# Attention scores and outputs of a unit in two blocks on TensorE instead of in pairs of heads

## The chip, the cores and the metric

One Trainium2 chip, one core. The metric is the time on the device in microseconds (us), the median of several runs. All runs told here were fast (granted TensorE clock 0.998 to 1.0). Before: 256.43 us (256.35 to 256.56, 3 runs).

## The reference

A sparse attention feeds a gated feed-forward block. Batch 4, 8 heads, 768 positions, head size 64.

```python
def _attn_ref(q, k, v):
    block, window = (32, 16)
    k_sum = k.reshape(B, H, nb, block, D).max(axis=3)        # 24 block keys
    v_sum = v.reshape(B, H, nb, block, D).mean(axis=3)
    scores_l = scale * q @ k.T          # kept where |i - j| < window
    scores_s = scale * q @ k_sum.T + log(block)
    a = softmax(concat([scores_l masked, scores_s]))
    return a @ concat([v, v_sum])

def _moe_ref(x, w_gate, w_val, w_out, w_res):               # x: 3072 x 512, d_ff 1536
    ffn_out = gelu(x @ w_gate) * (x @ w_val) @ w_out
    return x + sigmoid(x @ w_res) * ffn_out
```

## The kernel before

The 3072 rows are worked in eight units of 384 (half a batch each), numbered 0 to 7. A unit has 12 gate and value tiles (names g, vv, product gvT), then three row tiles of residual gate (r, th) and of the second feed-forward matmul (f, 12 steps each). While unit u does its r and f, the attention of unit u + 1 is slipped in: scores s, exp and mask to P, attention output ao, normalized xn, and xn turned to xT for the next unit's matmuls. I call that stretch the boundary of unit u + 1. PSUM, the memory from which the other engines read TensorE's results, has four rotating banks `ps_mm`, a two-bank tile `ps_s`, and one bank each in `ps_t` and `ps_o`.

One head pair (hp), of four:

```python
        def s_step(u, hp, st, banks=None, tiles=None):
            if tiles:
                s, banks = tiles, True
            elif banks:
                s = [p.tile([128, 512], F32, tag=tag, name="s") for p, tag in banks]
            else:
                s2 = ps_s.tile([128, 2, 512], F32, tag="s", name="s")
                s = [s2[:, hh] for hh in range(2)]
            s_mm(u, hp, [x[:, 0:TU] for x in s])
            P = ppool.tile([128, 2, HT, QT], BF16, tag="P", name="P")
            if banks:
                for hh in range(2):
                    nc.scalar.activation(P[:, hh].rearrange("p t q -> p (t q)"), s[hh][:, 0:TU], AF.Exp,
                                         scale=scale, bias=bias_t[:])
            else:
                nc.scalar.activation(P.rearrange("p a t q -> p a (t q)"), s2[:, :, 0:TU], AF.Exp,
                                     scale=scale, bias=bias_t[:])
            if u:
                Pf = P.rearrange("p a t q -> p (a t) q")
                nc.vector.tensor_mul(Pf, Pf, maskt.unsqueeze(1).to_broadcast([128, 2 * HT, QT]))
            st["P", hp] = P

        def av_step(u, hp, st, pool=ps_o, tag="ao"):
            b, half = u // 2, u % 2
            P = st["P", hp]
            ao = pool.tile([128, NSUB, 2, D + 1], F32, tag=tag, name="ao")
            for sub in range(NSUB):
                for hh in range(2):
                    for e in range(2):
                        t = 2 * sub + e
                        nc.tensor.matmul(ao[64 * e:64 * e + 64, sub, hh, :], P[:, hh, t, :],
                                         vext[b % 2][:, half * HT + t, 2 * hp + hh, 0:D + 1],
                                         start=True, stop=True, skip_group_check=True)
            av_end(hp, st, ao)
# ...
        def av_end(hp, st, ao):
            rz = work.tile([128, NSUB, 2, 1], F32, tag="rz", name="rz")
            nc.vector.reciprocal(rz[:], ao[:, :, :, D:D + 1])
            xn = st["xn"][:, hp].rearrange("p s (h d) -> p s h d", d=D)
            nc.vector.tensor_mul(xn, ao[:, :, :, 0:D], rz.to_broadcast([128, NSUB, 2, D]))

        def xt_step(u, ko, st, pool, tag, copy=nc.vector.tensor_copy):
            xp = pool.tile([128, TU], BF16, tag=tag, name="xp")
            for sub in range(NSUB):
                nc.tensor.transpose(xp[:, sub * 128:(sub + 1) * 128],
                                    st["xn"][:, ko, sub, :], ident[:])
            copy(st["xT"][:, ko, :], xp[:])

        def xt_dma(ko, st):
            nc.sync.dma_start_transpose(out=st["xT"][:, ko].rearrange("d (s k) -> d s k", k=128),
                                        in_=st["xn"][:, ko].rearrange("p s d -> p (s d)"))
```

The order at a boundary (`st` is the unit that ends, `nst` the one that comes). Unit 1 has the first order, units 2 to 7 the second:

```python
        def first_out(u, st, gvT, nst):
            n = u + 1
            other = dict(pool=ps_t, tag="t")
            turn = dict(pool=ps_t, tag="t", copy=nc.scalar.copy)
            s_step(n, 0, nst)
            s_step(n, 1, nst, TO2)
            for sub in range(NSUB):
                res_step(st, sub)
            ffn_step(st, gvT, 0, 0, 4)
            av_step(n, 0, nst)
            av_step(n, 1, nst, **other)
            s_step(n, 2, nst)
            ffn_step(st, gvT, 1, 0, 4)
            ffn_step(st, gvT, 2, 0, 4)
            ffn_step(st, gvT, 0, 4, 8)
            xt_step(n, 0, nst, **turn)
            av_step(n, 2, nst)
            s_step(n, 3, nst)
            ffn_step(st, gvT, 1, 4, 8)
            ffn_step(st, gvT, 2, 4, 8)
            ffn_step(st, gvT, 0, 8, FO)
            xt_step(n, 1, nst, **turn)
            av_step(n, 3, nst)
            ffn_step(st, gvT, 1, 8, FO)
            xt_step(n, 2, nst, **turn)
            xt_step(n, 3, nst, ps_o, "ao")
            end_step(u, st, 0)
            ffn_step(st, gvT, 2, 8, FO)
            end_step(u, st, 1)
            end_step(u, st, 2)

        def mid_out(u, st, gvT, nst):
            n = u + 1
            other = dict(pool=ps_t, tag="t")
            s_step(n, 0, nst)
            s_step(n, 1, nst, TO2)
            res_step(st, 0)
            res_step(st, 1)
            ffn_step(st, gvT, 0, 0, 4)
            av_step(n, 0, nst)
            xt_dma(0, nst)
            av_step(n, 1, nst, **other)
            xt_dma(1, nst)
            s_step(n, 2, nst)
            s_step(n, 3, nst, MM2)
            if n % 2 == 0:
                pool_after(nst["P", 3][0:1, 0, 0, 0:1])
                for i in range(2, 4):
                    vsum_bc(n // 2, 3 * i, 3 * i + 3, nc.gpsimd)
            ffn_step(st, gvT, 0, 4, FO)
            ffn_step(st, gvT, 1, 0, 3)
            av_step(n, 2, nst)
            xt_dma(2, nst)
            av_step(n, 3, nst, **other)
            xt_dma(3, nst)
            end_step(u, st, 0)
            ffn_step(st, gvT, 1, 3, FO)
            res_step(st, 2)
            end_step(u, st, 1)
            ffn_step(st, gvT, 2, 0, FO)
            end_step(u, st, 2)
```

The softmax here doesn't subtract the row's maximum and nothing guards it: scores larger than these inputs give would overflow.

Of the kernel before, what the change touches and what calls it, by code (L numbers as in the profile page):

```python
# [8 lines left out]
F32 = mybir.dt.float32  # L9
BF16 = mybir.dt.bfloat16  # L10
AF = mybir.ActivationFunctionType
# [4 lines left out]
def kernel(  # L16
# [11 lines left out]
    nc = tc.nc  # L28
# [25 lines left out]
    wpool = ctx.enter_context(tc.tile_pool(name="wpool", bufs=1))  # L54
    qk = ctx.enter_context(tc.tile_pool(name="qk", bufs=1))
    work = ctx.enter_context(tc.tile_pool(name="work", bufs=3))
    ppool = ctx.enter_context(tc.tile_pool(name="ppool", bufs=4))
    upool = ctx.enter_context(tc.tile_pool(name="upool", bufs=2))
    ps_mm = ctx.enter_context(tc.tile_pool(name="ps_mm", bufs=4, space=bass.MemoryType.PSUM))
    ps_s = ctx.enter_context(tc.tile_pool(name="ps_s", bufs=1, space=bass.MemoryType.PSUM))  # L60
# [17 lines left out]
    q_nat = const.tile([128, NQ, DM], BF16, name="q_nat")  # L78
    vext = [const.tile([128, NT, H, VP], BF16, name=f"vext{i}") for i in range(2)]
    vsum = [const.tile([128, DM], BF16, name=f"vsum{i}") for i in range(2)]  # L80
    vpart = const.tile([128, DM], BF16, name="vpart")
    w_gate = wpool.tile([128, KO, DFF], BF16, name="w_gate")
    w_val = wpool.tile([128, KO, DFF], BF16, name="w_val")
# [55 lines left out]
    with tc.manual_schedule():  # L139
# [182 lines left out]
# [6 lines that stand above are left out]
                s2 = ps_s.tile([128, 2, 512], F32, tag="s", name="s")  # L328
                s = [s2[:, hh] for hh in range(2)]
            s_mm(u, hp, [x[:, 0:TU] for x in s])  # L330
            P = ppool.tile([128, 2, HT, QT], BF16, tag="P", name="P")
            if banks:
                for hh in range(2):
                    nc.scalar.activation(P[:, hh].rearrange("p t q -> p (t q)"), s[hh][:, 0:TU], AF.Exp,  # L334
                                         scale=scale, bias=bias_t[:])
            else:
                nc.scalar.activation(P.rearrange("p a t q -> p a (t q)"), s2[:, :, 0:TU], AF.Exp,  # L337
                                     scale=scale, bias=bias_t[:])
            if u:
                Pf = P.rearrange("p a t q -> p (a t) q")  # L340
                nc.vector.tensor_mul(Pf, Pf, maskt.unsqueeze(1).to_broadcast([128, 2 * HT, QT]))  # L341
            st["P", hp] = P

        MM2 = ((ps_mm, "mm"),) * 2
        TO2 = ((ps_t, "t"), (ps_o, "ao"))
# [13 lines that stand above are left out]
# [18 lines left out]
# [10 lines that stand above are left out]
# [6 lines left out]
        def gv_mm(ps, w, st, fo, kos):  # L393
            for ko in kos:
                nc.tensor.matmul(ps[:, 0:TU], w[:, ko, fo * 128:(fo + 1) * 128], st["xT"][:, ko, :],  # L395
                                 start=(ko == 0), stop=(ko == KO - 1), skip_group_check=True)

        def gv_end(gvT, fo, g, vv):
            ge = work.tile([128, TU], F32, tag="ge", name="ge")
            nc.scalar.activation(ge[:], g[:, 0:TU], AF.Gelu)  # L400
            nc.vector.tensor_mul(gvT[:, fo, :], ge[:], vv[:, 0:TU])  # L401

        def mm_tile(name):
            return ps_mm.tile([128, 512], F32, tag="mm", name=name)
# [13 lines left out]
            gv_end(gvT, 0, g, vv)  # L418

        def fo_last_two(st, gvT):  # L420
            g = [mm_tile("g"), mm_tile("g")]
            for i in range(2):
                gv_mm(g[i], w_gate, st, FO - 2 + i, range(KO))
            for i in range(2):
                vv = mm_tile("vv")
                gv_mm(vv, w_val, st, FO - 2 + i, range(KO))
                gv_end(gvT, FO - 2 + i, g[i], vv)

        def res_step(st, sub):
            ss = slice(sub * 128, (sub + 1) * 128)  # L430
            r = mm_tile("r")
            for ko in range(KO):
                nc.tensor.matmul(r[:], st["xT"][:, ko, ss], w_res[:, ko, :],  # L433
                                 start=(ko == 0), stop=(ko == KO - 1))
            st["th", sub] = work.tile([128, DM], F32, tag="th", name="th")
            nc.scalar.activation(st["th", sub][:], r[:], AF.Tanh, scale=0.5)  # L436

        def ffn_step(st, gvT, sub, lo, hi):
            ss = slice(sub * 128, (sub + 1) * 128)
            if lo == 0:  # L440
                st["f", sub] = mm_tile("f")
            for fo in range(lo, hi):
                nc.tensor.matmul(st["f", sub][:], gvT[:, fo, ss], w_out[:, fo, :],  # L443
                                 start=(fo == 0), stop=(fo == FO - 1), skip_group_check=True)
# [13 lines left out]
        def end_step(u, st, sub):  # L458
            end_part(u, st, sub, st["f", sub], slice(0, DM))
# [122 lines left out]
        def pool_after(x):  # L582
            nc.gpsimd.tensor_copy(gate2[:], x)

        def first_out(u, st, gvT, nst):
            n = u + 1
            other = dict(pool=ps_t, tag="t")
            turn = dict(pool=ps_t, tag="t", copy=nc.scalar.copy)
            s_step(n, 0, nst)
            s_step(n, 1, nst, TO2)  # L590
            for sub in range(NSUB):
                res_step(st, sub)
            ffn_step(st, gvT, 0, 0, 4)
            av_step(n, 0, nst)
            av_step(n, 1, nst, **other)
            s_step(n, 2, nst)
            ffn_step(st, gvT, 1, 0, 4)
            ffn_step(st, gvT, 2, 0, 4)
            ffn_step(st, gvT, 0, 4, 8)
            xt_step(n, 0, nst, **turn)  # L600
            av_step(n, 2, nst)
            s_step(n, 3, nst)
            ffn_step(st, gvT, 1, 4, 8)
            ffn_step(st, gvT, 2, 4, 8)
            ffn_step(st, gvT, 0, 8, FO)
            xt_step(n, 1, nst, **turn)
            av_step(n, 3, nst)
            ffn_step(st, gvT, 1, 8, FO)
            xt_step(n, 2, nst, **turn)
            xt_step(n, 3, nst, ps_o, "ao")  # L610
            end_step(u, st, 0)
            ffn_step(st, gvT, 2, 8, FO)
            end_step(u, st, 1)
            end_step(u, st, 2)

        def mid_out(u, st, gvT, nst):
            n = u + 1
            other = dict(pool=ps_t, tag="t")
            s_step(n, 0, nst)
            s_step(n, 1, nst, TO2)  # L620
            res_step(st, 0)
            res_step(st, 1)
            ffn_step(st, gvT, 0, 0, 4)
            av_step(n, 0, nst)
            xt_dma(0, nst)
            av_step(n, 1, nst, **other)
            xt_dma(1, nst)
            s_step(n, 2, nst)
            s_step(n, 3, nst, MM2)
            if n % 2 == 0:  # L630
                pool_after(nst["P", 3][0:1, 0, 0, 0:1])
                for i in range(2, 4):
                    vsum_bc(n // 2, 3 * i, 3 * i + 3, nc.gpsimd)
            ffn_step(st, gvT, 0, 4, FO)
            ffn_step(st, gvT, 1, 0, 3)
            av_step(n, 2, nst)
            xt_dma(2, nst)
            av_step(n, 3, nst, **other)
            xt_dma(3, nst)
            end_step(u, st, 0)  # L640
            ffn_step(st, gvT, 1, 3, FO)
            res_step(st, 2)
            end_step(u, st, 1)
            ffn_step(st, gvT, 2, 0, FO)
            end_step(u, st, 2)
# [101 lines left out]
```

## Time and profile before

| | before |
|---|---|
| time, median | 256.43 us |
| span of the profiled run | 254.6 us |
| TensorE busy | 97% |
| boundary of unit 1, first s to first g of unit 1 | 13.50 us |
| first s of unit 2 to first s of unit 3 | 28.19 us |

The busy time of each engine in two stretches, the two of the last rows of the table. Columns: the stretch, its length, then busy us and number of instructions of TensorE (PE), its weight loads (PEld), VectorE, ScalarE and GpSimd; then granted clock, DMA share and GB/s:

```profile
38.15:51.65 13.50, 13.24 (x155) 7.17 (x158) 6.92 (x18) 8.13 (x13) 4.68 (x6) 1.00 1.63 190
69.79:97.98 28.19, 27.93 (x238) 15.58 (x241) 15.98 (x31) 13.72 (x24) 15.86 (x21) 1.00 1.16 109
```

TensorE has no idle time to speak of in either, and the others are half idle. Yet "busy" counts a matmul from its start to its modelled end, with the pipeline's overlap.

### The profile page before, as it was taken

What the parts mean: (1) busy time and instruction counts of PE and PEld (TensorE: products, weight loads), DVE (VectorE), ACT (ScalarE), POOL (GpSimd) and SP (SyncE); (2) the same over time, 40 slices, a digit from 0 to 9 for tenths busy, and PEclk for the clock granted to TensorE, in tenths of its full rate; (3) what the DMA queues carried; (4) which work ended last, traced back from release to release, by engine and by line L of the source; (5) the groups of instructions that cost most, each with busy time, mean ns of one, the idle gap of its engine ahead of it and who ended that gap; (6) DMA issues with size and microseconds to landing.
All of it is one profiled execution on the core that took longest, in us unless ns stands there. A gap on an engine that the chain in (4) does not pass through costs nothing.

```text
span 254.6 us, 5847 instructions
## 1 busy us (share of the span) xinstructions
PE 246.6 (97%) x2303; PEld 139.7 (55%) x2328; DVE 159.4 (63%) x364; ACT 129.6 (51%) x216; POOL 97.3 (38%) x128
## 2 busy tenths in 40 slices
PE   6999999999999999999999999999999999999994
PEld 2676555565545665446544665446545555456544
DVE  6985796397667544858567544958567544854424
ACT  8885468366572337353572337254572337353320
POOL 8895542361506970274406970274404000000000
PEclk9999999999999999999999999999999999999999
DMA  5999999999404999399404999289604400230003
GB/s 80 177 182 197 197 205 207 175 176 222 61 19 121 159 150 150 56 161 171 103 18 120 162 155 153 49 162 170 104 18 115 98 3 0 50 139 0 3 1 124
DMA packets 98107, 29.34 MB, mean 115 GB/s; under 512 B 83224, under 2 KB 94944, under 8 KB 97984
## 3 DMA queue, kind: packets, MB, share of 16 engines
q0 software_dynamic: 68352, 14.76, 66.3%
q1 hardware_dynamic: 29728, 14.21, 25.7%
q8 instruction: 18, 0.29, 0.5%
q14 instruction: 9, 0.07, 0.1%
HBM read 29.36 MB, written 6.29 MB: 140 GB/s over the span
## 4 chain that ended last, share of the span: by engine, by line
PE 93%; DVE 5%; issue 2%; DVEq 0%
PE g L395 25%; PE vv L395 24%; PE f L443 23%; PE r L433 8%; PE s L317 3%; PE ao L355 3%; PE vs L282 1%; PE ao L367 1%; PE tp L220 1%; PE vs L290 1%; DVE ks L237 1%; PE xp L380 1%; DVE o L452 1%; DVE th L449 1%; PE gv L395 1%
## 5 line engine op out<-in xcount | busy, mean ns | idle before, releaser
L401 DVE TENSOR_TENSOR gvT<-ge,vv 128x384 bf16<-128x384 f32 x95 | 52.2, 552 | 48.1 <-PE vv L395 43.9
L400 ACT ACTIVATE ge<-g 128x384 f32<-128x384 f32 x95 | 46.7, 491 | 67.3 <-DVE gvT L401 34.8
L395 PE MATMUL g<-xT,w_gate 128*128 128x384 bf16 x380 | 78.0, 326 | 0.0
L395 PE MATMUL vv<-xT,w_val 128*128 128x384 bf16 x380 | 77.8, 326 | 0.0
L443 PE MATMUL f<-w_out,gvT 128*128 128x512 bf16 x262 | 62.7, 379 | 1.5 <-issue 1.1
L395 PEld LDWEIGHTS <-w_gate 128*128 128x128 bf16 x384 | 37.1, 98 | 26.2 <-issue 1.4
L395 PEld LDWEIGHTS <-w_val 128*128 128x128 bf16 x384 | 37.6, 98 | 24.7
L443 PEld LDWEIGHTS <-gvT 128*128 128x128 bf16 x276 | 25.7, 98 | 29.5
L107 POOL DMA_DIRECT2D vext<-in_v_dram x32 | 24.1, 777 | 15.0 <-DMA w_out<-in_moe_w_out_dram 5.6
L436 ACT ACTIVATE th<-r 128x512 f32<-128x512 f32 x24 | 13.5, 607 | 27.6 <-PE r L433 27.6
L449 DVE SCALAR_TENSOR_TENSOR th<-th,f 128x512 f32<-128x512 f32 (+2 forms) x26 | 16.6, 640 | 14.4 <-PE f L443 14.4
L341 DVE TENSOR_TENSOR P<-P,maskt 128x768 bf16<-128x768 bf16 x28 | 16.2, 580 | 11.0 <-ACT P L337 6.1
L433 PE MATMUL r<-w_res,xT 128*128 128x512 bf16 x88 | 22.7, 380 | 0.4
L302 POOL COPY vext<-vsum 32x1536 bf16<-32x1536 bf16 x12 | 17.2, 1464 | 13.0 <-DMA vsum<-vpart 12.9
L452 DVE SCALAR_TENSOR_TENSOR o<-th,xn 128x512 f32<-128x512 f32 (+2 forms) x26 | 18.2, 701 | 0.9
L375 DVE TENSOR_TENSOR xn<-ao,rz 128x384 bf16<-128x384 f32 x32 | 17.8, 557 | 1.1
L337 ACT ACTIVATE P<-s,bias_t 128x768 bf16<-128x768 f32 x17 | 15.3, 901 | 4.5 <-PE s L317 4.3
L127 POOL DMA_DIRECT2D q_nat<-in_q_dram x18 | 15.8, 899 | 0.9 <-issue 0.7
L334 ACT ACTIVATE P<-s,bias_t 128x384 bf16<-128x384 f32 x30 | 15.7, 579 | 0.0
L237 DVE TENSOR_REDUCE ks<-kW 128x24 bf16<-128x768 bf16 x16 | 15.1, 943 | 0.0
L433 PEld LDWEIGHTS <-xT 128*128 128x128 bf16 x96 | 8.8, 98 | 9.9
L373 DVE RECIPROCAL rz<-ao 128x6 f32<-128x6 f32 x32 | 6.1, 191 | 10.9 <-PE ao L355 10.0
(90 smaller groups left out, 187.1 us busy)
## 6 DMA issues: line engine op xcount, KB each, us to landing
out_dram<-o SPq DMA_DIRECT2D x23, 256.0 KB, 2.2
vext<-in_v_dram POOLq DMA_DIRECT2D x32, 96.0 KB, 6.4
q_nat<-in_q_dram POOLq DMA_DIRECT2D x18, 128.0 KB, 6.4
w_gate<-in_moe_w_gate_dram POOLq DMA_DIRECT2D x6, 256.0 KB, 8.9
w_val<-in_moe_w_val_dram POOLq DMA_DIRECT2D x6, 256.0 KB, 9.3
w_out<-in_moe_w_out_dram POOLq DMA_DIRECT2D x3, 512.0 KB, 14.4
k_nat<-in_k_dram POOLq DMA_DIRECT2D x16, 96.0 KB, 5.8
vext<-vext SPq DMA_DIRECT2D x6, 144.0 KB, 5.4
```

Of the source, the lines that this page charges most:

```text
L107: nc.gpsimd.dma_start(out=vext[b % 2][0:QT, :, h, 0:D], in_=v[b, h].rearrange("(t p) d -> p t d", p=QT))
L237: nc.vector.tensor_reduce(out=ks.rearrange("d (t n) -> d t n", n=2), in_=kw[:, :, 0:QT].rearrange("d t (n w) -> d t n w", w=BLK), axis=myb ...
L302: eng.tensor_copy(vext[b % 2][96:128, lo:hi, :, 0:D], src)
L341: nc.vector.tensor_mul(Pf, Pf, maskt.unsqueeze(1).to_broadcast([128, 2 * HT, QT]))
L375: nc.vector.tensor_mul(xn, ao[:, :, :, 0:D], rz.to_broadcast([128, NSUB, 2, D]))
L395: nc.tensor.matmul(ps[:, 0:TU], w[:, ko, fo * 128:(fo + 1) * 128], st["xT"][:, ko, :], start=(ko == 0), stop=(ko == KO - 1), skip_group_ch ...
L400: nc.scalar.activation(ge[:], g[:, 0:TU], AF.Gelu)
L401: nc.vector.tensor_mul(gvT[:, fo, :], ge[:], vv[:, 0:TU])
L433: nc.tensor.matmul(r[:], st["xT"][:, ko, ss], w_res[:, ko, :], start=(ko == 0), stop=(ko == KO - 1))
L443: nc.tensor.matmul(st["f", sub][:], gvT[:, fo, ss], w_out[:, fo, :], start=(fo == 0), stop=(fo == FO - 1), skip_group_check=True)
L449: nc.vector.scalar_tensor_tensor(th[:, cs], th[:, cs], 1.0, f[:, 0:n], ALU.add, ALU.mult)
L452: nc.vector.scalar_tensor_tensor(o.rearrange("p (k d) -> p k d", d=128), th[:, cs].rearrange("p (k d) -> p k d", d=128), 0.5, x, ALU.mult, ...
```

## The change

All scores of a unit are computed in one place: 24 (head pair, query tile) columns in three groups of eight, each filling two banks with 512 columns. All attention outputs are computed in a second place. The aim is to change less often between TensorE's kinds of work. P becomes one tile `p_all` of the whole unit. In unit 1, where x is turned by TensorE, the four transposes stand together. The gelus of the last two tiles are recorded ahead of the value matmuls. Cut to its core:

```diff
+        def s_all(u):
+            # three groups: banks of ps_mm, of ps_s, of ps_t and ps_o
+            for i in range(3):
+                ...
+                for j in range(8):
+                    hp, t = divmod(8 * i + j, HT)
+                    for hh in range(2):
+                        nc.tensor.matmul(s[hh][:, j * QT:(j + 1) * QT], kw[ps, tt, hp, :], ...)
+                ... # exp of 512 columns a bank (1024 in group 1), mask of 512 a head
+        def av_all(u, st):
+            for hp in range(NP):
+                ... # ao: ps_t, ps_o, then the two halves of ps_s; av_end after hp 0, 1 and 3
+                if u > 1: xt_dma(i, st)
         def first_out(u, st, gvT, nst):
+            s_all(n)
+            res_step(st, 0)
+            res_step(st, 1)
+            for lo in (0, 4):
+                for sub in range(2):
+                    ffn_step(st, gvT, sub, lo, lo + 4)
+            av_all(n, nst)
+            for sub in range(2):
+                ffn_step(st, gvT, sub, 8, FO)
+                end_step(u, st, sub)
+            res_step(st, 2)
+            ffn_step(st, gvT, 2, 0, 4)
+            xt_step(n, 0, nst, ps_t, "t", nc.scalar.copy)
+            xt_step(n, 1, nst, ps_o, "ao")
+            xt_step(n, 2, nst, ps_t, "t", nc.scalar.copy)
+            xt_step(n, 3, nst, ps_o, "ao")
+            ffn_step(st, gvT, 2, 4, FO)
             end_step(u, st, 2)
         def mid_out(u, st, gvT, nst):
+            s_all(n)
+            ... # block sums of v to GpSimd, as before
             res_step(st, 0)
             res_step(st, 1)
+            ffn_step(st, gvT, 0, 0, FO)
+            av_all(n, nst)
             end_step(u, st, 0)
+            ffn_step(st, gvT, 1, 0, FO)
             res_step(st, 2)
             end_step(u, st, 1)
             ffn_step(st, gvT, 2, 0, FO)
```

More of the change, by code (lines that the diff above doesn't have):

```diff
@@ L56 @@
     work = ctx.enter_context(tc.tile_pool(name="work", bufs=3))
-    ppool = ctx.enter_context(tc.tile_pool(name="ppool", bufs=4))
     upool = ctx.enter_context(tc.tile_pool(name="upool", bufs=2))
@@ L80 @@
     vsum = [const.tile([128, DM], BF16, name=f"vsum{i}") for i in range(2)]
+    p_all = const.tile([128, 2, NP * HT, QT], BF16, name="p_all")
     vpart = const.tile([128, DM], BF16, name="vpart")
@@ L330, in s_step @@
             s_mm(u, hp, [x[:, 0:TU] for x in s])
-            P = ppool.tile([128, 2, HT, QT], BF16, tag="P", name="P")
+            P = p_all[:, :, hp * HT:(hp + 1) * HT]
             if banks:
@@ L339, in s_step @@
             if u:
-                Pf = P.rearrange("p a t q -> p (a t) q")
-                nc.vector.tensor_mul(Pf, Pf, maskt.unsqueeze(1).to_broadcast([128, 2 * HT, QT]))
+                nc.vector.tensor_mul(P, P, maskt.unsqueeze(1).unsqueeze(1).to_broadcast([128, 2, HT, QT]))
             st["P", hp] = P
+        def s_all(u):
+            b, half = u // 2, u % 2
+            kw, qt = kW[b % 2], qT[b % 2]
+            s2 = None
+            for i in range(3):
+                if i == 0:
+                    s = [ps_mm.tile([128, 512], F32, tag="mm", name="s") for _ in range(2)]
+                elif i == 1:
+                    s2 = ps_s.tile([128, 2, 512], F32, tag="s", name="s")
+                    s = [s2[:, hh] for hh in range(2)]
+                else:
+                    s = [p.tile([128, 512], F32, tag=tag, name="s") for p, tag in TO2]
+                for j in range(8):
+                    hp, t = divmod(8 * i + j, HT)
+                    tt = half * HT + t
+                    for hh in range(2):
+                        ps = slice(hh * 64, hh * 64 + 64)
+                        nc.tensor.matmul(s[hh][:, j * QT:(j + 1) * QT], kw[ps, tt, hp, :],
+                                         qt[ps, tt // 2, hp, (tt % 2) * QT:(tt % 2 + 1) * QT],
+                                         start=True, stop=True, skip_group_check=True)
+                js = slice(8 * i, 8 * i + 8)
+                m = maskt.unsqueeze(1).to_broadcast([128, 8, QT])
+                for hh in range(1 if i == 1 else 2):
+                    if i == 1:
+                        nc.scalar.activation(p_all[:, :, js].rearrange("p a j q -> p a (j q)"), s2[:], AF.Exp,
+                                             scale=scale, bias=bias_t[:])
+                    else:
+                        nc.scalar.activation(p_all[:, hh, js].rearrange("p j q -> p (j q)"), s[hh][:], AF.Exp,
+                                             scale=scale, bias=bias_t[:])
+                for hh in range(2):
+                    nc.vector.tensor_mul(p_all[:, hh, js], p_all[:, hh, js], m)
@@ new lines, in av_all @@
+        def av_all(u, st):
+            b, half = u // 2, u % 2
+            aos = []
+            for hp in range(NP):
+                if hp < 2:
+                    pool, tag = TO2[hp]
+                    ao = pool.tile([128, NSUB, 2, D + 1], F32, tag=tag, name="ao")
+                else:
+                    if hp == 2:
+                        s2 = ps_s.tile([128, 2, 512], F32, tag="s", name="ao")
+                    ao = s2[:, hp - 2, 0:NSUB * 2 * (D + 1)].rearrange("p (s h d) -> p s h d", s=NSUB, h=2)
+                for sub in range(NSUB):
+                    for hh in range(2):
+                        for e in range(2):
+                            t = 2 * sub + e
+                            nc.tensor.matmul(ao[64 * e:64 * e + 64, sub, hh, :], p_all[:, hh, hp * HT + t, :],
+                                             vext[b % 2][:, half * HT + t, 2 * hp + hh, 0:D + 1],
+                                             start=True, stop=True, skip_group_check=True)
+                aos.append(ao)
+                if hp != 2:
+                    for i in range(2 if hp == 3 else hp, hp + 1):
+                        av_end(i, st, aos[i])
+                        if u > 1:
+                            xt_dma(i, st)
@@ L420, in fo_last_two @@
         def fo_last_two(st, gvT):
-            g = [mm_tile("g"), mm_tile("g")]
+            ge = []
             for i in range(2):
-                gv_mm(g[i], w_gate, st, FO - 2 + i, range(KO))
+                g = mm_tile("g")
+                gv_mm(g, w_gate, st, FO - 2 + i, range(KO))
+                ge.append(work.tile([128, TU], F32, tag="ge", name="ge"))
+                nc.scalar.activation(ge[i][:], g[:, 0:TU], AF.Gelu)
             for i in range(2):
@@ L426, in fo_last_two @@
                 gv_mm(vv, w_val, st, FO - 2 + i, range(KO))
-                gv_end(gvT, FO - 2 + i, g[i], vv)
+                nc.vector.tensor_mul(gvT[:, FO - 2 + i, :], ge[i][:], vv[:, 0:TU])
         def res_step(st, sub):
@@ L586, in first_out @@
             n = u + 1
-            other = dict(pool=ps_t, tag="t")
-            turn = dict(pool=ps_t, tag="t", copy=nc.scalar.copy)
-            s_step(n, 0, nst)
-            s_step(n, 1, nst, TO2)
-            for sub in range(NSUB):
-                res_step(st, sub)
-            ffn_step(st, gvT, 0, 0, 4)
-            av_step(n, 0, nst)
-            av_step(n, 1, nst, **other)
-            s_step(n, 2, nst)
-            ffn_step(st, gvT, 1, 0, 4)
-            ffn_step(st, gvT, 2, 0, 4)
-            ffn_step(st, gvT, 0, 4, 8)
-            xt_step(n, 0, nst, **turn)
-            av_step(n, 2, nst)
-            s_step(n, 3, nst)
-            ffn_step(st, gvT, 1, 4, 8)
-            ffn_step(st, gvT, 2, 4, 8)
-            ffn_step(st, gvT, 0, 8, FO)
-            xt_step(n, 1, nst, **turn)
-            av_step(n, 3, nst)
-            ffn_step(st, gvT, 1, 8, FO)
-            xt_step(n, 2, nst, **turn)
+            s_all(n)
[9 more added lines that the diff above has]
+            res_step(st, 2)
+            ffn_step(st, gvT, 2, 0, 4)
+            xt_step(n, 0, nst, ps_t, "t", nc.scalar.copy)
+            xt_step(n, 1, nst, ps_o, "ao")
+            xt_step(n, 2, nst, ps_t, "t", nc.scalar.copy)
             xt_step(n, 3, nst, ps_o, "ao")
-            end_step(u, st, 0)
-            ffn_step(st, gvT, 2, 8, FO)
-            end_step(u, st, 1)
+            ffn_step(st, gvT, 2, 4, FO)
             end_step(u, st, 2)
@@ L617, in mid_out @@
             n = u + 1
-            other = dict(pool=ps_t, tag="t")
-            s_step(n, 0, nst)
-            s_step(n, 1, nst, TO2)
+            s_all(n)
+            if n % 2 == 0:
+                pool_after(p_all[0:1, 1, 4 * HT - 1, 0:1])
+                for i in range(2, 4):
+                    vsum_bc(n // 2, 3 * i, 3 * i + 3, nc.gpsimd)
             res_step(st, 0)
             res_step(st, 1)
-            ffn_step(st, gvT, 0, 0, 4)
-            av_step(n, 0, nst)
-            xt_dma(0, nst)
-            av_step(n, 1, nst, **other)
-            xt_dma(1, nst)
-            s_step(n, 2, nst)
-            s_step(n, 3, nst, MM2)
-            if n % 2 == 0:
-                pool_after(nst["P", 3][0:1, 0, 0, 0:1])
-                for i in range(2, 4):
-                    vsum_bc(n // 2, 3 * i, 3 * i + 3, nc.gpsimd)
-            ffn_step(st, gvT, 0, 4, FO)
-            ffn_step(st, gvT, 1, 0, 3)
-            av_step(n, 2, nst)
-            xt_dma(2, nst)
-            av_step(n, 3, nst, **other)
-            xt_dma(3, nst)
+            ffn_step(st, gvT, 0, 0, FO)
+            av_all(n, nst)
             end_step(u, st, 0)
-            ffn_step(st, gvT, 1, 3, FO)
+            ffn_step(st, gvT, 1, 0, FO)
             res_step(st, 2)
```

## The prediction

> **What bounds the kernel now.** I read the page's busy times and its chain first, then the order in time of TensorE around one unit boundary, then the queues that feed it.
>
> ```profile
> PE 246.6 (97%) x2303; PEld 139.7 (55%) x2328; DVE 159.4 (63%) x364; ACT 129.6 (51%) x216; POOL 97.3 (38%) x128
> ...
> ## 4 chain that ended last, share of the span: by engine, by line
> PE 93%; DVE 5%; issue 2%; DVEq 0%
> ```
>
> TensorE is busy 97% of the span and carries 93% of the chain. The other engines have room; they matter only where they make TensorE wait. So the change is worth what it removes from TensorE's own sequence, less the waits it puts in. Busy time alone does not say that TensorE does useful work: its pace has to be read from start to start. Here is the boundary of unit 4 (columns: start, duration, engine, line, operation):
>
> ```profile
> 127.04 0.52 PE L317 MATMUL s<-qT,kW 64*128 64x64 bf16 x24
> 127.50 1.90 PE L433 MATMUL r<-w_res,xT 128*128 128x512 bf16 x7
> 129.23 1.03 PE L443 MATMUL f<-w_out,gvT 128*128 128x512 bf16 x4
> 130.19 0.57 PE L355 MATMUL ao<-vext,P 128*64 128x65 bf16 x24
> 130.69 0.53 PE L317 MATMUL s<-qT,kW 64*128 64x64 bf16 x24
> 131.38 2.32 PE L443 MATMUL f<-w_out,gvT 128*128 128x512 bf16 x10 [0.16 <-issue]
> 133.63 0.57 PE L355 MATMUL ao<-vext,P 128*64 128x65 bf16 x24
> 134.13 2.12 PE L443 MATMUL f<-w_out,gvT 128*128 128x512 bf16 x9
> ```
>
> Two things are to be seen. The small matmuls are few microseconds in all. And the weight tile changes shape at every border: 128*128 for f, r, g and vv, 64*128 for s, 128*64 for ao. There are seven borders per unit boundary: vv/s, s/r, f/ao, ao/s, s/f, f/ao, ao/f. (The count x10 before "issue" is eleven matmuls of which one record is missing.) Unit 1's boundary shows what a border costs, because it has shorter blocks:
>
> ```profile
> 45.55 0.33 PE L380 MATMUL xp<-ident,xn 128*128 128x128 bf16 x3
> 45.81 0.38 PE L355 MATMUL ao<-vext,P 128*64 128x65 bf16 x12
> 46.12 0.35 PE L317 MATMUL s<-qT,kW 64*128 64x64 bf16 x12
> 46.40 2.76 PE L443 MATMUL f<-w_out,gvT 128*128 128x512 bf16 x12
> ...
> 50.45 0.50 PE L380 MATMUL xp<-ident,xn 128*128 128x128 bf16 x6
> 50.78 1.03 PE L443 MATMUL f<-w_out,gvT 128*128 128x512 bf16 x4
> ```
>
> From start to start, 12 s take 0.28 us and 24 take 0.46: 0.015 each and 0.10 for leaving the block. 12 ao take 0.31, 24 take 0.50: 0.016 each and 0.12 for leaving. On the way in, three xp take 0.26 before ao where six take 0.33 before f, so 0.055 each and 0.095 for the border; and f x4 takes 0.96 before ao where four at 0.216 are 0.86. Every border costs 0.10 to 0.11 us.
>
> **What the Trainium skill says.** "TensorEngine Tiling (Array Packing)", Key Properties: changing the tiling mode, not just the tile, drains TensorE. The trace agrees and gives the price just derived. "TensorE: Matmul & The Clock Gate", section "Wait — 56ns, not 53.3ns?": warm back-to-back matmuls start N / 2.4 GHz + 2.5 ns apart, 215.7 ns at N = 512; f and r here run at 0.216, so they have nothing left to gain. The table at the top of that page gives ScalarE and VectorE a strict FIFO queue: a small copy cannot pass what was recorded ahead of it. "DMA: Bandwidth & Descriptors" has about 2.0 us of fixed time in a DMA; this trace has 2.3 us from issue to landing for the xT transposes.
>
> **The change, part by part.** The matmuls are the same in number (the built programs have 4658 TensorE rows each). What changes is their order.
>
> Units 2 to 7 (six boundaries): s in one block, ao in one block. Borders vv/s, s/r, f/ao, ao/f: four instead of seven. 3 x 0.105 x 6 = 1.9 us removed. One boundary (unit 5) also had ao wait 0.13 us for a masked P; that should go: 2.0 in all.
>
> Unit 1: borders go from ten (vv/s, s/r, f/ao, ao/s, s/f, xp/ao, ao/s, s/f, xp/ao, ao/f) to four: 6 x 0.105 = 0.6 us removed.
>
> ScalarE and VectorE do the same exps and masks in 512-wide pieces: 5 activations for 6 and 6 masks for 4. Is P ready for the one ao block? With s at time 0: the exp table load ends at 0.6 (127.64 in unit 4). A 384-wide exp repeats after 0.46 and a 768-wide one after 0.80, so 0.88 ns a column: 0.58 for 512, 1.02 for 1024. The last exp ends near 0.6 + 4 x 0.58 + 1.02 + 0.1 = 4.05, the last mask (below the 0.56 of 768 columns) near 4.5. TensorE reaches ao at 0.81 (s) + 8 x 0.216 (r) + 12 x 0.216 (f) + 0.1 = 5.2. So 0.7 us spare. The six score banks were free before too. Gelu ahead of both vv is the order ScalarE has already; no gain there.
>
> What it adds in unit 1. Call the start of ao T. The four xT transposes on TensorE now stand together, after ao (0.11 + 48 x 0.016 = 0.9) and 16 matmuls at 0.216 (3.46), so from T + 4.35. They alternate between two banks, so the third waits for ScalarE's copy of the first (0.48) and the fourth for VectorE's copy of the second. VectorE's queue, in the order of the built program, is four reciprocal-and-multiply pairs, then both end steps, then that copy:
>
> ```profile
> 130.61 0.20 DVE L373 RECIPROCAL rz<-ao 128x6 f32<-128x6 f32 x1 [0.53 <-PE ao L355]
> ...
> 131.32 0.18 DVE L373 RECIPROCAL rz<-ao 128x6 f32<-128x6 f32 x1
> ```
>
> ```profile
> 51.26 0.68 DVE L449 SCALAR_TENSOR_TENSOR th<-th,f 128x512 f32<-128x512 f32 x1
> ...
> 53.90 0.68 DVE L449 SCALAR_TENSOR_TENSOR th<-th,f 128x512 f32<-128x512 f32 x1
> ```
>
> A pair repeats after 0.71 and starts 0.42 after the first ao (130.61 against 130.19); two end steps take 2.64. So the copy starts at T + 0.42 + 4 x 0.71 + 2.64 = T + 5.9, takes 0.36 (its row in the trace), and TensorE ends the fourth transpose near T + 6.5. Without waiting it would be T + 4.35 + 12 x 0.055 = T + 5.0. Cost 1.45 us, all on TensorE's path, since w_out's matmuls stand behind it.
>
> What it adds in units 2 to 7. xT is turned by DMA, four issues on one queue, which come 1.28 us apart at best and land 2.3 after issue:
>
> ```profile
> 105.82 2.48 SPq L385 DMA_TRANSPOSE xT<-xn  x2
> ```
>
> ```profile
> xT<-xn SPq DMA_TRANSPOSE x2, 2.3
> ```
>
> Before, two of them went out early, behind the first ao. Now all four follow the one ao block: first xn at T + 0.42 + 0.23 + 0.56 = T + 1.2, issue T + 1.35, fourth issue T + 5.2, landed T + 7.5. TensorE asks for the fourth after ao 0.9, f 2.59, r 0.86, f 2.59 and six gate and value matmuls at 0.1625 (0.98): T + 7.9. The spare time falls from 2.0 us (landed 138.5, asked for at 140.51 in unit 4) to 0.4. Three of the six first issues before took 1.8 to 2.1 us instead of 1.2; such an issue would make TensorE wait about 0.2 to 0.4. I allow 0.5 us over six units.
>
> Sum: 256.43 - 2.0 - 0.6 + 1.45 + 0.5 = 255.8. The per-block slopes give a little more saving (0.33 a unit instead of 0.315), so I say 255.6.
>
> **Rivals.** (1) The transposes' queue becomes the bound: if fourth xT lands 0.5 to 1 us late in each unit, 3 to 6 us come back and the kernel is slower, near 259 to 261. For it: issue and landing are serial and the margin is 0.4. Against: the spacing of 1.28 and the landing of 2.3 hold wherever the DMA rings were quiet, and they are quiet at that time. (2) The wait in unit 1 does not occur or is shorter, because VectorE gets to the copy earlier: then 254.3 to 255. Against: the queue order is fixed in the build and VectorE's durations are steady. (3) Unit 1 asks for w_out earlier: its second third landed 14.4 us after its issue at 27.86, at 42.27, and would be first used at 38.15 + 0.82 + 16 x 0.216 = 42.4. A later landing adds its lateness once, some tenths. (4) Borders are not saved because the longer blocks starve on P or on banks: 256.5 and above; the 0.7 us of spare time speaks against it.
>
> **Range and chances.** The saving of 2.6 is well measured (it could be 2.3 to 2.8). The wait in unit 1 is 0.6 (ScalarE's copy alone) to 1.8. The transposes cost 0 to 1.5. Together 254.6 to 256.9. Two per cent are 5.1 us; nothing but rival 1 in full comes near: faster 0.5%, slower 1.5%.
>
> **What would show it.** Right: four blocks per boundary, s x48 near 0.81 us and ao x48 near 0.9 from start to start; boundaries of units 2 to 7 shorter by some 0.3; unit 1's boundary longer by 0.6 to 1.0 (13.50 us before, from 38.15 to 51.65), with TensorE idle before the fourth xp, released by VectorE's copy; fourth xT landing 0 to 0.5 us ahead of use. Wrong: gaps before the fourth gate matmul in each unit (rival 1), gaps before ao released by P (rival 4), or boundaries that shrink by less than 0.2 although the borders are gone.

## The result, and the profile after

255.62 us (255.53 to 255.88, 4 runs) against 256.50 (256.35 to 256.77, 4 runs) of the kernel before in the same rounds. The ratio is 0.9966 (95% interval 0.9949 to 0.9984). Ratios here are the mean time of one kernel's fast runs over that of the other's of the same rounds, so not quite the ratio of the medians quoted. The interval lies below 1.

The two stretches of the kernel after that answer to those shown of before, same columns:

```profile
38.21:52.46 14.25, 13.15 (x158) 6.96 (x157) 9.40 (x23) 8.48 (x12) 5.74 (x8) 1.00 1.63 195
70.60:98.46 27.86, 27.86 (x241) 15.51 (x241) 15.71 (x33) 13.45 (x23) 15.21 (x20) 1.00 1.08 108
```

The later units are shorter by 0.33 us, and in the stretch shown TensorE is busy throughout. Unit 1's boundary is longer by 0.75, and there TensorE is idle for 1.1 of it. By stretches of the two traces, in us:

| from first s to first s | before | after | change |
|---|---|---|---|
| start to unit 1 | 38.15 | 38.21 | +0.06 |
| unit 1 to 2 | 31.64 | 32.39 | +0.75 |
| 2 to 3 | 28.19 | 27.86 | -0.33 |
| 3 to 4 | 29.06 | 28.72 | -0.34 |
| 4 to 5 | 28.19 | 27.86 | -0.33 |
| 5 to 6 | 29.18 | 28.72 | -0.46 |
| 6 to 7 | 28.19 | 28.06 | -0.13 |
| 7 to the end | 42.00 | 41.67 | -0.33 |

The sum is -1.11, the spans differ by 1.1 (254.6 and 253.5).

TensorE in order of time at the boundary of unit 4, the same place as in the prediction (start, duration, line, operation):

```profile
127.19 0.87 PE L360 MATMUL s<-qT,kW 64*128 64x64 bf16 x48
127.99 1.90 PE L492 MATMUL r<-w_res,xT 128*128 128x512 bf16 x8
129.73 2.75 PE L502 MATMUL f<-w_out,gvT 128*128 128x512 bf16 x12
132.41 0.95 PE L390 MATMUL ao<-vext,p_all 128*64 128x65 bf16 x48
133.29 2.76 PE L502 MATMUL f<-w_out,gvT 128*128 128x512 bf16 x12
...
140.32 0.33 PE L451 MATMUL g<-xT,w_gate 128*128 128x384 bf16 x1
```

A border is a place where TensorE goes from matmuls of one weight shape to those of another (128*128, 64*128, 128*64). Here there are four where there were seven. From start to start s x48 takes 0.80 us and ao x48 0.88. Where the work changes but not the shape there is no such price: the eight r before f take 1.74 us to the first f (127.99 to 129.73), 0.2175 each, against 0.216 inside a block. In the last line TensorE takes up the fourth part of xT at 140.32 without a wait; it had landed at 139.97 by the trace's record of its DMA.

The transposes of unit 1 on TensorE, where a bracket tells the idle time before and what ended it:

```profile
48.65 0.50 PE L436 MATMUL xp<-ident,xn 128*128 128x128 bf16 x6
49.54 0.33 PE L436 MATMUL xp<-ident,xn 128*128 128x128 bf16 x3 [0.40 <-DVE th L508]
50.57 0.33 PE L436 MATMUL xp<-ident,xn 128*128 128x128 bf16 x3 [0.70 <-DVE xT L438]
50.73 1.89 PE L502 MATMUL f<-w_out,gvT 128*128 128x512 bf16 x8
```

Twelve transposes take 2.09 us (48.647 to 50.733) where twelve back to back would take 0.67. The fourth group waits for VectorE's copy of the second. Why the copy is late is in VectorE's order of time:

```profile
48.84 0.68 DVE L508 SCALAR_TENSOR_TENSOR th<-th,f 128x512 f32<-128x512 f32 x1
49.56 0.69 DVE L511 SCALAR_TENSOR_TENSOR o<-th,xn 128x512 f32<-128x512 f32 x1
50.17 0.35 DVE L438 COPY xT<-xp 128x384 bf16<-128x384 bf16 x1
```

The transposes that it copies ended near 49.1; the copy starts at 50.17, straight after the second end step. (The bracket of the third group names VectorE's th. That is an inference from the last semaphore event; the trace has the third group waiting on the semaphore that ScalarE's copies raise, and the copy of the first part ran from 49.01 to 49.49. A bracket like this has to be checked against what the program waits for.)

```profile
49.01 0.48 ACT L438 COPY xT<-xp 128x384 bf16<-128x384 bf16 x1 [0.43 <-PE xp L436]
```

The chain of the kernel after, shares of the span:

```profile
PE 90%; DVE 7%; issue 1%; DMA 1%; DVEq 0%
```

There is now a DMA in it, which there was not before: the fourth transpose of xT in unit 6, from its issue to its landing:

```profile
194.75 2.32 DMA xT<-xn
```

One queue issues the four of a unit one after the other, in unit 4 in 5.08 us:

```profile
133.76 5.08 SPq L441 DMA_TRANSPOSE xT<-xn  x4
```

### The profile page after: what moved, and what is told of

Its sections match the earlier page's. It is cut to its first block, busy times and chain, and to the rows that moved or that the text cites. A ratio compares the mean times of both kernels' runs of the same rounds, so it can differ in the third digit from the quotient of the medians.

```text
span 253.5 us, 5885 instructions
## 1 busy us (share of the span) xinstructions
PE 246.7 (97%) x2328; PEld 139.2 (55%) x2328; DVE 158.9 (63%) x379; ACT 127.3 (50%) x209; POOL 96.2 (38%) x128
## 4 chain that ended last, share of the span: by engine, by line
PE 90%; DVE 7%; issue 1%; DMA 1%; DVEq 0%
PE g L451 25%; PE vv L451 24%; PE f L502 22%; PE r L492 8%; PE s L360 2%; PE ao L390 2%; DVE th L508 1%; PE vs L282 1%; DVE o L511 1%; PE tp L220 1%; PE ao L423 1%; DMA xT<-xn 1%; PE vs L290 1%; DVE ks L237 1%; PE wp L534 1%
## 5 line engine op out<-in xcount | busy, mean ns | idle before, releaser
L456 ACT ACTIVATE ge<-g 128x384 f32<-128x384 f32 x81 | 39.7, 490 | 62.4 <-PE g L451 32.8
L502 PE MATMUL f<-w_out,gvT 128*128 128x512 bf16 x276 | 63.4, 379 | 0.0
L502 PEld LDWEIGHTS <-gvT 128*128 128x128 bf16 x276 | 26.4, 98 | 31.0
L373 DVE TENSOR_TENSOR p_all<-p_all,maskt 128x512 bf16<-128x512 bf16 x42 | 16.6, 423 | 9.7 <-ACT p_all L370 5.2
L370 ACT ACTIVATE p_all<-s,bias_t 128x512 bf16<-128x512 f32 x28 | 17.8, 692 | 0.1
L511 DVE SCALAR_TENSOR_TENSOR o<-th,xn 128x512 f32<-128x512 f32 (+2 forms) x26 | 16.9, 651 | 0.9
L121 POOL DMA_DIRECT2D k_nat<-in_k_dram x16 | 12.0, 798 | 0.6 <-issue 0.6
```

The lines of the kernel that those rows point to most:

```text
L370: nc.scalar.activation(p_all[:, hh, js].rearrange("p j q -> p (j q)"), s[hh][:], AF.Exp, scale=scale, bias=bias_t[:])
L456: nc.scalar.activation(ge[:], g[:, 0:TU], AF.Gelu)
L502: nc.tensor.matmul(st["f", sub][:], gvT[:, fo, ss], w_out[:, fo, :], start=(fo == 0), stop=(fo == FO - 1), skip_group_check=True)
L511: nc.vector.scalar_tensor_tensor(o.rearrange("p (k d) -> p k d", d=128), th[:, cs].rearrange("p (k d) -> p k d", d=128), 0.5, x, ALU.mult, ...
```

## The experiments

Each kernel was timed in five rounds beside the kernel before; times are medians, ratios are to the kernel before. The changed kernel itself ran twice more as a yardstick (e1 and e11). All results were correct. The 95% intervals in brackets tell which lie clear of 1.

**e1: the changed kernel again.** No edit.

> The changed kernel once more, as the yardstick for the runs beside it. 255.6 us, 0.9 below the kernel before.

255.29 us (255.06 to 255.72), ratio 0.9959 (0.9947 to 0.9972). The kernel before in these rounds: 256.43. That is 1.14 below it where 0.9 was expected; the five runs of it spread over 0.66.

**e2: only units 2 to 7.** Undoes a part: unit 1's boundary has the order of before.

```diff
-            s_all(n)
-            ... (first_out of the change)
+            s_step(n, 0, nst)
+            s_step(n, 1, nst, TO2)
+            ... (first_out of the kernel before, on p_all)
```

> Only the boundaries of units 2 to 7 have the two blocks; unit 1's boundary is the old one. Theory (each border between weight shapes costs 0.105 us of TensorE, 18 of them go): 1.9 us below the kernel before, so 254.6. Rival (the gain is spread over both, or the DMA transposes take it back): 255.6 or more.

254.57 us (254.41 to 254.77), ratio 0.993 (0.9917 to 0.9942): 1.86 below the kernel before. The theory holds; the gain of the change is in these six boundaries and is larger than the gain of the whole.

**e3: only unit 1.** The counterpart.

```diff
-            s_all(n)
-            ... (mid_out of the change)
+            s_step(n, 0, nst)
+            s_step(n, 1, nst, TO2)
+            ... (mid_out of the kernel before, on p_all)
```

> Only unit 1's boundary has the new order; the others are the old ones. Theory (0.6 us of borders saved, 1.4 us of waiting for VectorE's copy added): 0.8 us above the kernel before, 257.3. Rival (unit 1's new order gains too, or is neutral): 255.9 to 256.5.

257.48 us (257.23 to 258.02), ratio 1.0047 (1.0033 to 1.006): 1.05 above the kernel before, 0.25 more than expected. Its trace has the boundary at 14.25 us (38.24 to 52.49), 0.75 over before, and the twelve transposes at 2.09; the span is 255.5, 0.9 over. So unit 1's new order is a loss, and e2 and e3 add up: -1.86 + 1.05 = -0.81, where the whole change gave -0.88 in the first rounds, -1.14 in e1 and -0.94 in e11. Time and span of e3 differ by 0.15, within the 0.8 us that its five runs spread over.

**e4: gelu order undone.** The last two tiles' gelus recorded as before.

```diff
-                ge.append(work.tile([128, TU], F32, tag="ge", name="ge"))
-                nc.scalar.activation(ge[i][:], g[:, 0:TU], AF.Gelu)
...
-                nc.vector.tensor_mul(gvT[:, FO - 2 + i, :], ge[i][:], vv[:, 0:TU])
+                gv_end(gvT, FO - 2 + i, g[i], vv)
```

> The changed kernel with the last two feed-forward tiles recorded as before (gelu after the value matmuls). Theory: ScalarE ran the gelus in that order anyway, so no change, within 0.1 us of the changed kernel. Rival (the early gelu frees the score banks sooner and part of the gain is its): up to 0.5 us slower than the changed kernel.

255.38 us (255.27 to 255.72), ratio 0.9964 (0.9952 to 0.9977), within 0.1 of e1 in the same rounds. That part of the change does nothing to the time.

**e5: unit 1's transposes into four banks.**

```diff
-            xt_step(n, 0, nst, ps_t, "t", nc.scalar.copy)
-            ... (four steps, two banks in turn)
+            x2 = ps_s.tile([128, 2, 1024], BF16, tag="s", name="xp")
+            xps = [ps_t tile, ps_o tile, x2[:, 0, 0:TU], x2[:, 1, 0:TU]]
+            for ko in range(KO):
+                ... # three transposes into xps[ko]
+                (nc.vector.tensor_copy if ko % 2 else nc.scalar.copy)(nst["xT"][:, ko, :], xps[ko][:, 0:TU])
```

> Unit 1's four transposes into four different banks, so that none waits for a copy; everything else as in the changed kernel. Theory (TensorE waits 1.4 us there for banks): 254.2 us, the twelve transposes 0.67 us from start to start instead of 2.09. Rival (the time there is lost to something else, such as the late multiplies that make x): no change, 255.6.

254.55 us (254.52 to 254.71), ratio 0.9928 (0.9915 to 0.994). Faster than the changed kernel, but 0.35 short of the expectation. TensorE at that place:

```profile
48.72 0.67 PE L663 MATMUL xp<-ident,xn 128*128 128x128 bf16 x9
49.99 0.33 PE L663 MATMUL xp<-ident,xn 128*128 128x128 bf16 x3 [0.61 <-ACT xT L664]
```

The fourth group still waits, now for ScalarE's copy of the third. The third and fourth groups are halves of one two-bank tile, and with the copy recorded in between, the build put a wait for ScalarE on the fourth. By the order of the program the fourth bank is free, so the wait is one of bookkeeping; that the tile counts as one buffer is inferred from this. So this run did not remove what it was meant to remove, and e9 mends it.

**e6: end steps later.** Same two banks as in the change; unit 0's two end steps recorded after the transposes.

```diff
             for sub in range(2):
                 ffn_step(st, gvT, sub, 8, FO)
-                end_step(u, st, sub)
...
             xt_step(n, 3, nst, ps_o, "ao")
+            for sub in range(2):
+                end_step(u, st, sub)
```

> Same two banks, but unit 0's two end steps recorded after the four transposes, so that VectorE's copies come first in its queue. Theory: the fourth transpose no longer waits for VectorE, the third still waits for ScalarE's copy of the first (about 0.6 us); so 0.8 to 0.9 us below the changed kernel, 254.8. If ScalarE's copies were the wait: no change.

254.44 us (254.34 to 254.89), ratio 0.9925 (0.9912 to 0.9939): 1.88 below the kernel before of these rounds, about 0.9 below the changed kernel's usual distance, and 0.36 below the 254.8 expected. TensorE's line:

```profile
49.54 0.49 PE L436 MATMUL xp<-ident,xn 128*128 128x128 bf16 x6 [0.40 <-DVE xT L438]
```

The third and fourth group now run together: the fourth no longer waits, the third still starts 0.62 us after the last of the second group (48.92, 0.06 would be its pace). From first transpose to f it is 1.23 us instead of 2.09, which is the 0.86 that the theory asks for. Again the bracket names VectorE where the third group's semaphore is that of ScalarE's copies.

**e7: more borders.** The strongest test of the mechanism: the same instructions, three f matmuls moved into the ao block of units 2 to 7.

```diff
-            ffn_step(st, gvT, 0, 0, FO)
-            av_all(n, nst)
+            ffn_step(st, gvT, 0, 0, FO - 3)
+            av_all(n, nst, lambda i: ffn_step(st, gvT, 0, FO - 3 + i, FO - 2 + i))   # one f after head pairs 0, 1, 2
```

> In the boundaries of units 2 to 7 the ao block is cut in four by three of the f matmuls that stood before it: the same matmuls, exps, masks and copies, but six more borders in each of six boundaries. Theory: 36 x 0.105 = 3.8 us, less the 0.2 that unit 6 now waits for its last transpose (the DMAs start earlier): 3.6 above the changed kernel, 259.2. Rival (the gain came from the wider exps or from fewer waits between engines): within 0.3 us of the changed kernel.

259.29 us (259.22 to 259.3, 4 runs), ratio 1.0111 (1.0094 to 1.0127): 2.97 above the kernel before, so 3.9 above where the changed kernel lies (0.94 below it in e11). The boundary of unit 4:

```profile
133.04 0.38 PE L390 MATMUL ao<-vext,p_all 128*64 128x65 bf16 x12
133.35 0.39 PE L504 MATMUL f<-w_out,gvT 128*128 128x512 bf16 x1
133.67 0.38 PE L390 MATMUL ao<-vext,p_all 128*64 128x65 bf16 x12
133.98 0.39 PE L504 MATMUL f<-w_out,gvT 128*128 128x512 bf16 x1
134.30 0.38 PE L390 MATMUL ao<-vext,p_all 128*64 128x65 bf16 x12
```

A lone f takes 0.32 from start to start instead of 0.216, twelve ao take 0.31 where 12 of the long block would take 0.19 (the long block's slope of 0.016). From the first f to the end of ao it is 4.24 us (131.00 to 135.24) against 3.56 in the change (129.73 to 133.29): 0.68 for six borders, 0.113 each. 36 x 0.113 = 4.1, less the 0.21 that unit 6 had waited for its transpose: 3.9, as measured. In the trace each of these stretches is 0.67 or 0.68 longer than the changed kernel's 27.86 or 28.72, and none of it is a wait for P: the nine f before ao take 2.04 us, nine times 0.216 and a border, though the last mask ends only 0.09 before. The rival, that the gain came from wider exps or from fewer waits, is out: those are unchanged here, and 18 borders at 0.105, 1.89 us, account for e2's 1.86.

**e8: less time for the DMA.** The third r tile moved ahead of ao.

```diff
             ffn_step(st, gvT, 0, 0, FO)
+            res_step(st, 2)
             av_all(n, nst)
             end_step(u, st, 0)
             ffn_step(st, gvT, 1, 0, FO)
-            res_step(st, 2)
```

> In units 2 to 7 the last r tile (0.86 us of TensorE) is moved ahead of ao: the same work, but TensorE asks for the transposed x 0.86 us sooner after ao. Theory (the fourth DMA transpose lands 0.1 to 0.4 us ahead of its use in five units and late in one): TensorE waits 0.5 to 0.9 us in each, 3.9 us in all, 259.5. Rival (transposes have over 0.9 us to spare): no change, 255.6.

259.08 us (258.68 to 259.57), ratio 1.0104 (1.0088 to 1.012): 2.76 above the kernel before, 3.7 above the changed kernel's usual place. In the boundary of unit 4 TensorE waits for the DMA:

```profile
141.39 0.32 PE L451 MATMUL g<-xT,w_gate 128*128 128x384 bf16 x1 [0.54 <-DMA xT<-xn]
```

Over the six boundaries the g and vv of the first tile lose 0.52, 0.55, 0.70, 0.79, 0.94 and 0.62 us, 4.1 in all, of which 0.21 is in the changed kernel too. So the transposes had about 0.1 to 0.4 us to spare in the change, and the first rival of the prediction was close: with 0.86 us less in each unit it is the result.

**e9: four banks without the wait.** As e5, with all transposes recorded before the copies.

```diff
             for ko in range(KO):
                 ... # three transposes into xps[ko]
+            for ko in range(KO):
                 (nc.vector.tensor_copy if ko % 2 else nc.scalar.copy)(nst["xT"][:, ko, :], xps[ko][:, 0:TU])
```

> As e5, but all twelve transposes are recorded before the four copies. In e5 the fourth transpose still waited 0.83 us: its two-bank tile counted as one buffer, so it waited for ScalarE's copy of the third. Theory: that wait goes, the twelve take 0.67 us from start to start, 0.78 below e5: 253.8 us (1.5 below the changed kernel). Rival (VectorE's late copies of the second and fourth part of x then hold up unit 1's first gate matmuls): 254.3 or more.

254.14 us (254.0 to 254.21, 4 runs), ratio 0.9909 (0.9894 to 0.9924); 1.35 below e11 beside it, expected 1.5.

```profile
48.65 0.83 PE L663 MATMUL xp<-ident,xn 128*128 128x128 bf16 x12
```

The twelve take 0.67 from start to start. The f that follow ran on without a wait, and so did unit 1's first gate matmuls. The span, 252.1, is 1.4 below the change's. The stretch from unit 1 to unit 2 is 30.98 us, 1.42 below e11's 32.40. So the wait for banks in unit 1 was worth its 1.4 us on the path.

**e10: the best of both.** As e9, and r1 behind ao in units 2 to 7.

```diff
             res_step(st, 0)
-            res_step(st, 1)
             ffn_step(st, gvT, 0, 0, FO)
             av_all(n, nst)
+            res_step(st, 1)
             end_step(u, st, 0)
```

> As e9, and in units 2 to 7 the second r tile moved behind ao, which gives the DMA transposes 0.86 us more (the reverse of e8). Theory: the occasional waits for the fourth transpose (0.2 to 0.5 us in the changed kernel's runs) go, all else equal: 253.6 us, and less scatter between runs; P is still masked in time (spare time falls from 0.7 us to about 0.4 at the last head pair). Rival (P or a bank comes late when ao is asked for 0.86 us earlier): 254 to 255.5.

253.73 us (253.6 to 253.91, 4 runs), ratio 0.9894 (0.9881 to 0.9908): 2.7 below the kernel before and 1.76 below e11. In its trace no unit waits for xT, the fourth transpose lands 0.9 to 1.3 us before use, and P is in time (in unit 4 the last mask ends 0.47 before the last head pair's ao). The smaller scatter that was expected is not shown: four runs spread over 0.31, those of e9 over 0.21 and of e11 over 0.48. It is the fastest of all that were run, and beats both kernels. Its span, 251.8, is 2.8 below that of the kernel before, as much as all borders and the wait for P were worth (below).

**e11: the changed kernel beside e9 and e10.**

> The changed kernel again, beside e9 and e10 on the same chip: 255.3 to 255.6 us.

255.49 us (255.26 to 255.74), ratio 0.9963 (0.995 to 0.9975). As expected.

## Why the prediction was right

The time was foreseen to 0.02 us, 255.6 against 255.62, and that closeness is luck. The prediction's own sum is 255.78, and its correction of six times 0.015 gives 255.69, not 255.6. The terms read from the trace come to more: borders and the wait for P gave 2.8 us (2.6 foreseen), the wait in unit 1 cost 1.42 (1.45) and the DMA 0.21 (0.5), so the profiled span fell by 1.1. The median time fell by only 0.88; the 0.2 between is less than the runs' own spread of 0.35, and no run here explains it. (The prediction's 4658 rows stand in no page; the page after has 2328 matmuls and 2328 weight loads.) What counts is that each step can be checked.

- **TensorE is the bound, and a border costs 0.105 us.** Right. e2 gained 1.86 us (1.9 to 2.0 foreseen) with 18 borders fewer, e7 lost 3.9 with 36 more. The term was slightly small: 0.113 by e7's trace, 0.33 us for three borders in the units of the change, and 0.67 for six in unit 1 (0.75 longer with a wait of 1.42).
- **P is ready for the one ao block.** Right: in unit 4 the last mask ended at 131.67 (131.25 + 0.42) and ao began at 132.41, 0.74 us spare, with 0.7 foreseen. The wait of unit 5 for P is gone (its stretch fell by 0.46 instead of 0.33).
- **Unit 1 waits 1.45 us for the copies behind the end steps.** Right: 1.42 (2.09 - 0.67). T was 44.30; the copy was foreseen at T + 5.9 and began at 50.17, which is T + 5.87. e6 and e9 show the two halves of the wait: 0.86 for VectorE's order, the rest for the bank that ScalarE's copy holds. The boundary became 0.75 longer, foreseen 0.6 to 1.0.
- **The DMA transposes have 0.4 us to spare and cost about 0.5 us in all.** The margin was right, 0.12 to 0.39 in five units; the cost was 0.21 us, in unit 6, where the first issue took 1.72 us instead of 1.18, the case that was foreseen. e1's trace has 0.13 in unit 3 and 0.30 in unit 7 instead, so the place varies by run, and 0.2 to 0.4 is the size in the traces of the changed kernel. e8 shows that the margin is real.
- **The gelu order does nothing.** Right (e4).
- **w_out in unit 1.** Its second third landed at 42.00 and was used at about 42.5; no wait, so rival 3 did not occur, but by half a microsecond.

Open: the runs show what a border costs, not what TensorE does in that time. That it drains is the word of the Trainium skill's page "TensorEngine Tiling (Array Packing)", Key Properties; no run here takes it apart.

## What to carry to other kernels

When one engine is the bound and looks full, read starts, not busy time: a difference between a long and a short block of the same instruction gives the fixed price of entering and leaving it, and the number of borders times that price is what regrouping can gain. Regrouping bunches what follows, too: copies behind longer work in a queue that is worked in order, bank reuse, DMA issues in one queue. Count the spare time of each of these before and after, since here one of them ate 1.4 us of a gain of 2.8, and another had 0.4 us to spare and with 0.86 us less would have eaten more than the rest (e8).

## What the Trainium skill lacked or had wrong

- "TensorEngine Tiling (Array Packing)", Key Properties, says that a change of tiling mode drains TensorE, but gives no price. The runs show about 0.11 us for each change (0.095 to 0.12 by the slopes, 0.113 in e7), in and out, 128*128 to 64*128 or 128*64, and much the same between those two (ao x12 before s: 0.31 us).
- "TensorE: Matmul & The Clock Gate", section "Back-to-back issue gap", gives about 131 ns a matmul as the sustained rate of weight load and matmul pairs at N = 512, and calls N / 2.4 GHz + 2.5 ns an isolated gap that over-counts. Here sustained f and r at N = 512, each matmul with a weight load of its own (276 and 276 for f), ran at 216 ns from start to start, in all units, at a granted clock of 1.0: the value of the formula.
- "DMA: Bandwidth & Descriptors" has no issue spacing on trn2, in time, for DMA transposes of 128 x 384 from SBUF to SBUF on one queue, and its fixed cost is that of the GpSimd path. Here they came about 1.28 us apart and mostly landed 2.3 us after issue (up to 3.0 in unit 4); some first issues took 1.7 to 2.1 us instead of 1.2.
- No page that I read tells that a two-bank PSUM tile can count as one buffer for waits, which is inferred here: in e5 the second half waited for a copy of the first, and from e5 to e9 the twelve transposes fell from 1.44 to 0.67 us.
